# Cluster logits of batches 1 to 3 in paired columns, their low halves added by ScalarE and VectorE

## The chip, the cores and the metric

The program runs on one NeuronCore of a Trainium2 chip. The core has a matrix engine (TensorE, PE in the profile; its weight loads are shown apart as PEld), a vector engine (VectorE, DVE), a scalar engine (ScalarE, ACT), GpSimd (POOL) and a queue engine that issues transfers (SyncE, SP). All work in order, each on its own stream, and wait for one another through semaphores. The metric is the device time of one execution in microseconds, taken as a median of runs.

## The reference

```python
batch, n_heads, seq, head_dim = (4, 8, 768, 64); n_clusters = 16; n_tokens, d_model, d_ff = (3072, 512, 2048)

q_assign = np.argmax(np.einsum('bhsd,hcd->bhsc', q_n, c_n), axis=-1)   # q_n, k_n, c_n: rows scaled to unit norm
k_assign = np.argmax(np.einsum('bhsd,hcd->bhsc', k_n, c_n), axis=-1)
mask = q_assign[:, :, :, None] == k_assign[:, :, None, :]
scores = np.where(mask, scale * np.matmul(q, k.transpose(0, 1, 3, 2)), -1000000000.0)
attn = np.exp(scores - np.max(scores, axis=-1, keepdims=True))
attn = attn / (np.sum(attn, axis=-1, keepdims=True) + 1e-09)
x = np.matmul(attn, v)                          # heads side by side: 3072 tokens of 512
h = x @ w_in
P = a[0] + a[1] * h + a[2] * h ** 2 + a[3] * h ** 3
Q = 1.0 + np.abs(b[0]) * np.abs(h) + np.abs(b[1]) * h ** 2
out = (P / (Q + 1e-6)) @ w_out
```

Every row of q and of k is given to the nearest of its head's 16 centroids, and attention runs only between rows of one cluster. The products of rows and centroids, of which the largest is taken, are called logits here.

## The kernel before

All large products are made from 16-bit halves: a number is kept as a high part and a low part, and a product as two or three matmuls. The work goes by batch (4), by pair of heads (4 a batch) and by block of two tiles of 128 rows (3 a pair). For each pair `prep` loads q, k and v, scales and splits them (`tq1`, `tk1`), turns them by DMA or TensorE (`sq`, `sk`), makes the logits (`ptl`), finds each row's cluster and writes it as a mask into a second operand (`tq2`, `tk2`, turned into `sq`, `sk` again). `attend` then makes 12 score tiles `s` a pair (rows of 128 queries by 768 keys): four matmuls (L1277), the maximum on VectorE (L1292), the exponential and the copy `ah` on ScalarE (both by the helper at L546), the low half of `ah` on VectorE (L1312), a DMA that turns it (`at`), and 18 matmuls into `px` (L1331) for each. Batch 0 goes by keys instead (`z`, `at`, `px` at L1487 to L1512). `moe` works through a block of 256 tokens: `ph` (12 matmuls of 256 columns for each 128 of d_ff, L1639), a chain of elementwise steps on three engines (`u`, `t`, `s` again, a big buffer of that name), and `po` (6 matmuls of 512 columns, L1750).

Attention of batch b is woven into `moe` of batch b-1, and `moe` of batch 3 ends the program alone. The order is not found at run time: `ORDER` holds for each engine the list of operations by number, worked out beforehand; the plan only hands out buffers in that order. So an engine that waits holds up all that stands behind it in its list.

PSUM, into which TensorE writes, has eight banks, shared out in three rings. Ring `s` has two slots of two banks each, for score tiles. Ring `m` has two slots of one bank, for `ph`, `px`, the logits and small sums. Ring `o` has one slot of two banks, for `po`. A slot comes free when the last reader of its tile is done.

The logits of a pair (`logits`, L1158) are 48 matmuls into one `m` slot: for each of 24 tiles of 128 rows one of 16 columns with the centroids' high part, and one of 16 columns that adds the low part to it in PSUM. Behind them stand on VectorE the maximum `mx` (L1189) and the comparison `df` (L1190), which are the readers of the slot; a product on GpSimd (L1193), a second maximum (L1198) and a comparison (L1199) follow in SBUF. The tile `df` has one buffer. `wide_`, an older variant in `prep`, is off.

Of the kernel before, what the change touches and what calls it, by code (L numbers as in the profile page):

```python
# [10 lines left out]
F32 = mybir.dt.float32  # L11
F32R = mybir.dt.float32r
F16 = mybir.dt.float16
# [3 lines left out]
ALU = mybir.AluOpType  # L17
# [10 lines left out]
K = {'ghd': 0.0, 'rvp': 0, 'look': 62.89, 'mulp': 0.4, 'sub': 0, 'xn': 14, 'NR': 8, 'sgp': 1, 'scp': 1, 'vsc': 0.75, 'sup0': 0, 'stk': 2, 'lop': 0, 'mgp': 0, 'rvn': 2, 'tq2': 2, 'at': 3, 'es': 4, 'vn': 2, 'ah': 5, 'rel': 0, 'twin': 1, 'pet': '_01', 'avs': 3, 'ksum': 1, 'fst': '_0', 'hpa': 1}  # L28
# [348 lines left out]
def clustered_attention_moe_kernel(  # L377
# [66 lines left out]
    def kn(name, default=0.0):  # L444
        return K.get(name, default)

# [496 lines left out]
    def prep(b, hp, vt):  # L943
# [192 lines left out]
        for x in ("k1", "q1"):  # L1136
            turn(x, vt + kc("p2", b, 2), by_pe)

        G = 4 * NT
        wide_ = bool(kn("lgw", 0))  # L1140
        ptl = misc([P, G, NCL], F32, f"ptl{n}") if not wide_ else None
        if wide_:
            halves = [misc([P, G // 2, 2, NCL], F32, f"ptl{x}{n}") for x in "qk"]
# [725 lines left out]
```

## Time and profile before

| what | us |
|---|---|
| time, median of 3 runs (lowest, highest) | 896.92 (894.39, 898.39) |
| time of the profiled execution | 897.27 |
| its span, first to last instruction | 895.4 |
| TensorE busy, share of the span | 849.1, 95% |
| VectorE | 785.8, 88% |
| ScalarE | 755.2, 84% |
| GpSimd | 629.3, 70% |

The span is what the trace covers; the time holds 1.9 us more around it. The share is an average over unlike stages: the start (weights and batch 0, with little for TensorE to overlap), the woven stage of batches 1 to 3, and the last `moe`. So the profile is read stage by stage: how long each engine is busy there, and for whom TensorE waits.

### The profile page before, as it was taken

How to read it: one execution, taken by the hardware profiler on the slowest of the kernel's cores; microseconds unless marked ns; L12 is line 12 of the kernel's file. 1: busy time of each engine (PE TensorE's matmuls, PEld its weight loads, DVE VectorE, ACT ScalarE, POOL GpSimd, SP SyncE). 2: the span in 40 equal slices, each digit the busy share in tenths (PEclk: the TensorE clock that was granted, in tenths of full speed). 3: DMA queues.
4: the chain of work that ended last, by engine and by line, in shares of the span. 5: the costliest groups of instructions: out<-in, count | busy, mean ns of one | idle time of the engine just before them, and what ended most of it. 6: DMA issues, size and time to landing. Idle time of an engine off the chain costs nothing.

```text
span 895.4 us, 22725 instructions
## 1 busy us (share of the span) xinstructions
PE 849.1 (95%) x9045; PEld 597.8 (67%) x9045; DVE 785.8 (88%) x1388; ACT 755.2 (84%) x1050; POOL 629.3 (70%) x661
## 2 busy tenths in 40 slices
PE   2789999898999999999999999999999999999998
PEld 2557666675766777567776767777677666766664
DVE  7998979689989899999989998999889888876786
ACT  7557786899999989988999999998988898766674
POOL 1354685699988898778898988789988877422331
PEclk9899999999999999999999999999999999999999
DMA  8478755747989889999999799969888866300000
GB/s 278 138 170 198 190 161 144 206 96 145 194 166 217 159 163 213 188 191 197 167 220 175 154 186 179 180 133 214 144 159 126 160 126 113 87 1 25 7 25 25
DMA packets 364395, 134.70 MB, mean 150 GB/s; under 512 B 342144, under 2 KB 358528, under 8 KB 364288
## 3 DMA queue, kind: packets, MB, share of 16 engines
q1 hardware_dynamic: 364288, 133.24, 73.7%
q8 instruction: 71, 1.16, 0.5%
q14 instruction: 36, 0.29, 0.1%
HBM read 41.98 MB, written 6.29 MB: 54 GB/s over the span
## 4 chain that ended last, share of the span: by engine, by line
PE 55%; DVE 16%; ACT 11%; DMA 6%; issue 5%; POOL 5%; SPq 0%; ACTq 0%; DVEq 0%; POOLq 0%
PE po L1750 19%; PE ph L1639 17%; PE s L1277 6%; PE px L1331 5%; DVE top L1435 3%; ACT s L546 3%; DVE s L1292 3%; ACT u L546 2%; PE px L1506 2%; DVE ah L1312 2%; ACT ah L546 2%; PE z L1487 2%; DVE s L1732 1%; PE s L1408 1%; DMA rwi<-in_moe_w_in_dram 1%
## 5 line engine op out<-in xcount | busy, mean ns | idle before, releaser
L1639 PE MATMUL ph<-x,win 128*128 128x256 f16 x2304 | 267.6, 273 | 2.8 <-DVE xf L1357 1.2
L1750 PE MATMUL po<-wout,u 128*128 128x512 f16 x1152 | 268.6, 379 | 0.0
L1639 PEld LDWEIGHTS <-win 128*128 128x128 f16 x2304 | 223.2, 98 | 43.2 <-DVE xf L1357 3.5
L1679 POOL TENSOR_TENSOR s<-s,u 128x512 f32<-128x512 f32 x96 | 129.0, 1362 | 94.2 <-issue 52.6
L1750 PEld LDWEIGHTS <-u 128*128 128x128 f16 x1152 | 110.5, 98 | 115.3 <-issue 0.5
L1312 DVE SCALAR_TENSOR_TENSOR ah<-s,ah 128x768 f16<-128x768 f32 x144 | 136.1, 952 | 23.7 <-ACT ah L546 22.5
L1292 DVE TENSOR_SCALAR_CACHE_REDUCE s<-s,cc 128x768 f32<-128x768 f32 x144 | 145.2, 1019 | 9.3 <-PE s L1277 8.8
L546 ACT ACTIVATE s<-s,nm 128x768 f32<-128x768 f32 x144 | 125.4, 873 | 21.2 <-DVE s L1292 19.0
L1277 PE MATMUL s<-sk,sq 128*128 128x384 f16 x576 | 116.5, 329 | 4.1 <-DVE ah L1312 3.4
L546 ACT ACTIVATE ah<-s 128x768 f16<-128x768 f32 x144 | 115.9, 810 | 3.1
L1702 POOL TENSOR_TENSOR s<-s,u 128x512 f32<-128x512 f32 x72 | 102.0, 1429 | 16.9 <-ACT u L546 16.5
L1739 POOL TENSOR_TENSOR u<-s,u 128x512 f16<-128x512 f32 x72 | 86.4, 1207 | 30.9 <-DVE s L1732 14.5
L1331 PEld LDWEIGHTS <-at 128*128 128x128 f16 x2592 | 88.5, 98 | 13.6 <-issue 2.2
L1331 PE MATMUL px<-vhi,at 128*128 128x65 f16 x1728 | 91.1, 194 | 1.3 <-DMA at<-ah 0.8
L1331 PE MATMUL px<-vlo,at 128*128 128x64 f16 x864 | 86.8, 192 | 0.0
L1277 PEld LDWEIGHTS <-sq 128*128 128x128 f16 x576 | 52.9, 98 | 41.6 <-DVE ah L1312 8.7
L1660 DVE TENSOR_TENSOR t<-ph,t 128x512 f32<-128x512 f32 x96 | 65.4, 684 | 12.2 <-ACT t L546 11.7
L546 ACT ACTIVATE u<-ph 128x512 f32<-128x512 f32 x96 | 56.9, 595 | 21.8 <-PE ph L1639 21.3
L1732 DVE SCALAR_TENSOR_TENSOR s<-s,t 128x1024 f32<-128x1024 f32 (+1 forms) x49 | 63.0, 1286 | 1.4 <-POOL t L1716 0.6
L546 ACT ACTIVATE u<-t 128x1024 f16<-128x1024 f32 (+1 forms) x49 | 50.9, 1039 | 11.0 <-DVE t L1722 6.0
L546 ACT ACTIVATE t<-ph,gk 128x512 f32<-128x512 f32 x72 | 55.3, 774 | 0.0
L1665 DVE SCALAR_TENSOR_TENSOR t<-t,gk,ph 128x512 f32<-128x512 f32 x72 | 53.0, 742 | 1.1
(219 smaller groups left out, 1466.6 us busy)
## 6 DMA issues: line engine op xcount, KB each, us to landing
rwi<-in_moe_w_in_dram SPq DMA_DIRECT2D x16, 512.0 KB, 4.9
rwo<-in_moe_w_out_dram SPq DMA_DIRECT2D x16, 512.0 KB, 4.8
rk<-in_k_dram SPq DMA_DIRECT2D x32, 192.0 KB, 3.5
rq<-in_q_dram SPq DMA_DIRECT2D x32, 192.0 KB, 3.6
rvm<-in_v_dram SPq DMA_DIRECT2D x16, 384.0 KB, 4.1
rv<-in_v_dram SPq DMA_DIRECT2D x16, 384.0 KB, 4.6
out_dram<-ob SPq DMA_DIRECT2D x11, 512.0 KB, 3.8
at<-ah SPq DMA_TRANSPOSE x144, 4.1
```

Of the source, the lines that this page charges most:

```text
L546: lambda: nc.scalar.activation(out=out(), in_=in_(), func=func, **{a: (x() if callable(x) else x) for a, x in kw.items()}),
L1277: nc.tensor.matmul(sc.ap[:, i, :SH], lhsT=st["q" + x].ap[:, j, t, :], rhs=st["k" + x].ap[:, j, ks, :].rearrange("p t c -> p (t c)"), start ...
L1292: lambda nm=nm, view=view: ts(out=view(), in0=view(), scalar1=cc.ap, scalar2=None, op0=ALU.mult, op1=ALU.min, accum_out=nm.ap),
L1312: lambda part=part, view=view: stt(out=part(1), in0=view(), scalar=A_SCALE, in1=part(0), op0=ALU.mult, op1=ALU.subtract),
L1331: nc.tensor.matmul(px.ap[:, i, :w_], lhsT=at.ap[:, p_, kt, :], rhs=vv.ap[:, j, kt, :w_], start=(kt == 0 and vv is vhi and p_ == 0), stop=( ...
L1639: nc.tensor.matmul(ph[i].ap[:, fi * TW : (fi + 1) * TW], lhsT=win[f // 4][:, wpart, c, f % 4 * P : (f % 4 + 1) * P], rhs=xs[c].ap[:, xpart ...
L1660: lambda i=i, th=th, ph=ph: tt(out=th[i].ap, in0=ph[i].ap, in1=th[i].ap, op=ALU.mult),
L1679: lambda i=i, sh=sh, uh=uh: nc.gpsimd.tensor_tensor(out=sh[i].ap, in0=sh[i].ap, in1=uh[i].ap, op=ALU.mult),
L1702: lambda i=i, sh=sh, uh=uh: nc.gpsimd.tensor_tensor(out=sh[i].ap, in0=sh[i].ap, in1=uh[i].ap, op=ALU.mult),
L1732: lambda tw=tw, sw=sw: stt(out=sw(), in0=sw(), scalar=2.0, in1=tw(), op0=ALU.subtract, op1=ALU.mult),
L1739: lambda i=i, sh=sh, gl=gl, g16=g16, e=(nc.vector if gld else nc.gpsimd): e.tensor_tensor(out=gl[i].ap, in0=sh[i].ap, in1=g16()[:, 0, i * ...
L1750: nc.tensor.matmul(po[ti].ap, lhsT=g16()[:, part, c0 : c0 + P], rhs=wout[f // 4][:, wpart, f % 4], start=(k == 0 and f == f_first), stop=( ...
```

## The change

For batches 1 to 3 (`lgb`), each of the 24 tiles has one matmul of 32 columns instead of two of 16: its moving operand holds the high and the low part of the centroids side by side, and both results lie side by side in PSUM. The sum that PSUM made by itself is now made by two new steps: ScalarE copies the 384 low halves out of PSUM into the buffer of `df` as 16-bit numbers, and VectorE adds them to the high halves, in place in PSUM. The maximum and the comparison read the sums there, every second group of 16.

The tile grows from one bank to two and moves from ring `m` to ring `s`, the one of the score tiles. Batch 0 stays as it was. The variant `wide_` goes, and all five lists of `ORDER` are new.

```diff
-K = {..., 'hpa': 1}
+K = {..., 'hpa': 1, 'lgb': '123'}
...
-        ptl = misc([P, G, NCL], F32, f"ptl{n}") if not wide_ else None
+        paired = str(b) in kn("lgb", "")
+        if paired:
+            ptl = bank([P, 2, 512], F32, "s", f"ptl{n}", 2)
+        else:
+            ptl = misc([P, G, NCL], F32, f"ptl{n}")
+
+        def parts(i):
+            return ptl.ap[:, :, : G * NCL].rearrange("p x (g s c) -> p x g s c", s=2, c=NCL)[:, :, :, i]
+
+        def sums_():
+            return parts(0) if paired else ptl.ap.rearrange("p (x g) c -> p x g c", x=2)
...
         def logits():
             for g, (x, part) in enumerate((("q1", 1), ("q1", 1), ("k1", 2), ("k1", 2))):
                 for t in range(NT):
+                    if paired:
+                        nc.tensor.matmul(
+                            ptl.ap[:, g // 2, (g % 2 * NT + t) * 2 * NCL : (g % 2 * NT + t + 1) * 2 * NCL].rearrange("p (s c) -> p s c", s=2),
+                            lhsT=st[x].ap[:, g % 2, t, :], rhs=cen.ap[:, 0 : part + 1 : part, h0 + g % 2, :],
+                            start=True, stop=True,
+                        )
+                        continue
                     for i in (0, part):
...
-            op("PE", 1205, logits, [cen, st["q1"], st["k1"]], [ptl], vt + kc("p25", b, 2.5), [df], chain="logits")
+        u = vt + kc("p25", b, 2.5)
+        op("PE", 645 if paired else 1205, logits, [cen, st["q1"], st["k1"]], [ptl], u, [df], chain="logits")
+        if paired:
+            act(ac(384, 0, True), lambda: over_rows(df.ap).bitcast(F16), lambda: parts(1), AF.Copy, [ptl], [df], u)
+            dve(465, lambda: tt(out=parts(0), in0=parts(0), in1=over_rows(df.ap).bitcast(F16), op=ALU.add), [df], [ptl], u)
...
-        dve(465, lambda: nc.vector.tensor_reduce(out=mx.ap, in_=ptl.ap, axis=AX.X, op=ALU.max), [ptl], [mx], u)
-        dve(463, lambda: tt(out=df.ap, in0=ptl.ap, in1=spread(mx), op=ALU.is_ge), [ptl, mx], [df], u)
+        dve(465, lambda: nc.vector.tensor_reduce(out=mx.ap.rearrange("p (x g) -> p x g", x=2), in_=sums_(), axis=AX.X, op=ALU.max), [ptl], [mx], u)
+        dve(463, lambda: tt(out=over_rows(df.ap), in0=sums_(), in1=over_rows(spread(mx)), op=ALU.is_ge), [ptl, mx], [df], u)
```

How the new lists stand shows at the logits of batch 2's second pair of heads (`ptl_1`). In the names the first number is the pair of heads (for `ph`, `po` and `u` the block of tokens), the last one only numbers the buffer; L1158 is L1160 in the new file, L1277 is L1273, L1292 is L1288.

TensorE there, before; the logits stand right ahead of a score tile, and the `ph` behind it takes the other `m` slot:

```order
L1158 MATMUL ptl_1_5990<-cen,sq_1_5869 128x16
...
L1158 MATMUL ptl_1_5990<-cen,sk_1_5884 128x16
...
L1277 MATMUL s_0_0_1_6049<-sk_0_5240,sq_0_5483 128x384
...
L1639 MATMUL ph_0_4_0_6057<-x_0_0_3689,win_120 128x256
...
L1277 MATMUL s_0_1_0_6106<-sk_0_5240,sq_0_5483 128x384
```

and now, a `ph` and a `po` standing between the logits and the next two score tiles:

```order
L1160 MATMUL ptl_1_5877<-cen,sq_1_5772 128x32
...
L1160 MATMUL ptl_1_5877<-cen,sk_1_5757 128x32
...
L1635 MATMUL ph_0_4_0_5906<-x_0_0_3675,win_120 128x256
...
L1746 MATMUL po_2_1_5708<-wout_126,u_2_12_5359 128x512
...
L1273 MATMUL s_0_0_1_5945<-sk_0_5156,sq_0_5172 128x384
...
L1273 MATMUL s_0_1_0_5955<-sk_0_5156,sq_0_5172 128x384
```

Both score tiles moved behind `ph` and `po`; the logits are now a third guest of the two slots that they share.

ScalarE at the same place, now; the copy of the low halves is the row `df_1`:

```order
L547 ACTIVATE ah_3_5_1_5777<-s_3_5_1_5744 128x768
L547 ACTIVATE u_0_0_5664<-s_0_0_5723 128x1024
L547 ACTIVATE u_0_0_5664<-u_0_0_5664 128x1024
L547 ACTIVATE df_1_5920<-ptl_1_5877 128x384
L547 ACTIVATE s_0_0_0_5782<-s_0_0_0_5782,nm_0_0_0_5874 128x2x384
L547 ACTIVATE ah_0_0_0_5936<-s_0_0_0_5782 128x768
```

It stands behind two steps of `moe` over 1024 columns and ahead of the exponential of the score tile that was written before the logits.

VectorE at the same place, before:

```order
L1292 TENSOR_SCALAR s_0_0_0_5892,nm_0_0_0_5985<-s_0_0_0_5892,cc_0_5012 128x2x384
L1351 TENSOR_SCALAR inv_3_1_6042<-px_3_1_5903 128x4
L1354 RECIPROCAL inv_3_1_6042<-inv_3_1_6042 128x4
L1357 TENSOR_TENSOR xf_3_1_6046<-px_3_1_5903,inv_3_1_6042 128x256
L1189 TENSOR_REDUCE mx_1_6054<-ptl_1_5990 128x24
L1190 TENSOR_TENSOR df_1_6072<-ptl_1_5990,mx_1_6054 128x384
L1292 TENSOR_SCALAR s_0_0_1_6049,nm_0_0_1_6075<-s_0_0_1_6049,cc_0_5012 128x2x384
L1312 SCALAR_TENSOR_TENSOR ah_0_0_0_6070<-s_0_0_0_5892,ah_0_0_0_6070 128x768
```

and now, with the addition at L1179:

```order
L1288 TENSOR_SCALAR s_0_0_0_5782,nm_0_0_0_5874<-s_0_0_0_5782,cc_0_4940 128x2x384
L1347 TENSOR_SCALAR inv_3_1_5904<-px_3_1_5792 128x4
L1350 RECIPROCAL inv_3_1_5904<-inv_3_1_5904 128x4
L1353 TENSOR_TENSOR xf_3_1_5923<-px_3_1_5792,inv_3_1_5904 128x256
L1179 TENSOR_TENSOR ptl_1_5877<-ptl_1_5877,df_1_5920 128x2x12x16
L1185 TENSOR_REDUCE mx_1_5928<-ptl_1_5877 128x24
L1186 TENSOR_TENSOR df_1_5920<-ptl_1_5877,mx_1_5928 128x384
L1308 SCALAR_TENSOR_TENSOR ah_0_0_0_5936<-s_0_0_0_5782,ah_0_0_0_5936 128x768
L1288 TENSOR_SCALAR s_0_0_1_5945,nm_0_0_1_5961<-s_0_0_1_5945,cc_0_4940 128x2x384
```

The addition is put ahead of the maximum, the three readers of the slot stand together, and `ah` of the earlier score tile changes places with the maximum of the later one.

## Rows read from the trace of the kernel before

**Rows 1.** The page's first part: busy us, share, instructions of each engine.

```profile
PE 849.1 (95%) x9045; PEld 597.8 (67%) x9045; DVE 785.8 (88%) x1388; ACT 755.2 (84%) x1050; POOL 629.3 (70%) x661
```

**Rows 2.** Windows: stretch, its length, then busy us (instructions) of each engine.

```profile
0.00:200.00 200.00, 168.69 (x2035) 123.44 (x2035) 172.70 (x390) 151.84 (x253) 114.83 (x166) 0.98 0.65 176
200.00:400.00 200.00, 191.40 (x2132) 134.67 (x2121) 186.33 (x320) 185.50 (x253) 172.69 (x171) 0.99 0.96 180
350.00:400.00 50.00, 46.62 (x564) 33.00 (x562) 48.84 (x88) 46.30 (x63) 38.19 (x45) 1.00 1.06 190
400.00:760.00 360.00, 357.98 (x3902) 252.64 (x3901) 326.33 (x559) 329.22 (x439) 304.15 (x297) 1.00 0.91 165
760.00:895.40 135.40, 131.03 (x992) 87.01 (x990) 100.45 (x122) 88.67 (x108) 37.60 (x30) 1.00 0.11 29
```

**Rows 3.** The chain in order of time: start us, length us, what, and how many.

```profile
742.44 1.30 PE s L1277 x8
743.74 2.20 PE px L1331 x72
...
690.56 1.31 PE ph L1639 x12
...
859.84 5.24 PE ph L1639 x48
...
880.68 10.37 PE po L1750 x48
```

**Rows 4.** Windows, of the logits' line L1158 alone: PE busy (matmuls), PEld.

```profile
200.00:400.00 200.00, 5.40 (x192) 5.33 (x192) 0.99 0.96 180
400.00:760.00 360.00, 8.10 (x288) 7.92 (x288) 1.00 0.91 165
```

**Rows 5.** Timeline from 526 us: start, length, engine, line, what, [idle before].

```profile
526.37 0.75 PE L1158 MATMUL ptl<-cen,sq 128*128 128x16 f16 x24
526.97 0.75 PE L1158 MATMUL ptl<-cen,sk 128*128 128x16 f16 x24
527.57 1.45 PE L1750 MATMUL po<-wout,u 128*128 128x512 f16 x6
527.76 0.56 DVE L1189 TENSOR_REDUCE mx<-ptl 128x24 f32<-128x384 f32 x1
528.35 0.56 DVE L1190 TENSOR_TENSOR df<-ptl,mx 128x384 bf16<-128x384 f32 x1
```

**Rows 6.** Timeline from 573 us, the same columns.

```profile
573.70 0.74 PE L1158 MATMUL ptl<-cen,sq 128*128 128x16 f16 x24
...
577.08 0.55 DVE L1190 TENSOR_TENSOR df<-ptl,mx 128x384 bf16<-128x384 f32 x1
```

**Rows 7.** Groups of instructions: shapes, count | busy us, mean ns of one | idle before.

```profile
L546 ACT ACTIVATE rs<-px 128x256 f32<-128x256 f32 x12 | 4.5, 378 | 0.2 <-PE px L1549 0.2
L546 ACT ACTIVATE u<-ph 128x512 f32<-128x512 f32 x96 | 56.9, 595 | 21.8 <-PE ph L1639 21.3
L546 ACT ACTIVATE u<-u 128x1024 f32<-128x1024 f32 x47 | 49.5, 1054 | 0.9
L1190 DVE TENSOR_TENSOR df<-ptl,mx 128x384 bf16<-128x384 f32 x16 | 8.9, 555 | 0.3
L1660 DVE TENSOR_TENSOR t<-ph,t 128x512 f32<-128x512 f32 x96 | 65.4, 684 | 12.2 <-ACT t L546 11.7
```

**Rows 8.** Who TensorE waited for, whole span: us in total, times, longest.

```profile
PE vt L812 <- DVE vm L810: 2.5, 1, 2.5
PE ph L1639 <- DVE xf L1357: 1.2, 3, 0.7
PE ph L1639 <- DVE df L1190: 0.6, 1, 0.6
```

**Rows 9.** The same, from 200 to 760 us alone.

```profile
PE s L1277 <- DVE ah L1312: 3.4, 8, 0.9
PE px L1549 <- DVE rs L1541: 3.1, 1, 3.1
```

More of the change, by code (lines that the diff above doesn't have):

```diff
@@ L25 @@
 M_BIG, M_MID, M_LOW = 2.0 ** 15, 2.0 ** 7, 2.0 ** -4
-K = {'ghd': 0.0, 'rvp': 0, 'look': 62.89, 'mulp': 0.4, 'sub': 0, 'xn': 14, 'NR': 8, 'sgp': 1, 'scp': 1, 'vsc': 0.75, 'sup0': 0, 'stk': 2, 'lop': 0, 'mgp': 0, 'rvn': 2, 'tq2': 2, 'at': 3, 'es': 4, 'vn': 2, 'ah': 5, 'rel': 0, 'twin': 1, 'pet': '_01', 'avs': 3, 'ksum': 1, 'fst': '_0', 'hpa': 1}
+K = {'ghd': 0.0, 'rvp': 0, 'look': 62.89, 'mulp': 0.4, 'sub': 0, 'xn': 14, 'NR': 8, 'sgp': 1, 'scp': 1, 'vsc': 0.75, 'sup0': 0, 'stk': 2, 'lop': 0, 'mgp': 0, 'rvn': 2, 'tq2': 2, 'at': 3, 'es': 4, 'vn': 2, 'ah': 5, 'rel': 0, 'twin': 1, 'pet': '_01', 'avs': 3, 'ksum': 1, 'fst': '_0', 'hpa': 1, 'lgb': '123'}
 ORDER = {
     "ACT": """
[32 rows of a table removed]
[33 rows of a table added]
 """,
     "DVE": """
[37 rows of a table removed]
[37 rows of a table added]
 """,
     "PE": """
[28 rows of a table removed]
[28 rows of a table added]
 """,
     "POOL": """
[21 rows of a table removed]
[21 rows of a table added]
 """,
     "SP": """
[13 rows of a table removed]
[13 rows of a table added]
 """,
@@ L1139, in prep, with over_rows @@
         G = 4 * NT
-        wide_ = bool(kn("lgw", 0))
-        ptl = misc([P, G, NCL], F32, f"ptl{n}") if not wide_ else None
-        if wide_:
-            halves = [misc([P, G // 2, 2, NCL], F32, f"ptl{x}{n}") for x in "qk"]
-            def wide_logits(i):
-                x = ("q1", "k1")[i]
-                for g in range(2):
-                    for t in range(NT):
-                        nc.tensor.matmul(
-                            halves[i].ap[:, g * NT + t], lhsT=st[x].ap[:, g, t, :], rhs=cen.ap[:, 0 : 2 + i : 1 + i, h0 + g, :],
-                            start=True, stop=True,
-                        )
+        paired = str(b) in kn("lgb", "")
[7 more added lines that the diff above has]
+            return parts(0) if paired else ptl.ap.rearrange("p (x g) c -> p x g c", x=2)
+        def over_rows(a):
+            return a.rearrange("p (x g) c -> p x g c", x=2)
         def logits():
@@ L1165, in prep @@
         oh = df
-        if wide_:
-            ptl = buf([P, G, NCL], F32, "lsm", f"lsm{n}", 1)
-            for i, x in enumerate(("q1", "k1")):
-                op("PE", 610, lambda i=i: wide_logits(i), [cen, st[x]], [halves[i]], vt + kc("p25", b, 2.5), [df, ptl], chain="logits" + x)
-                low = buf([P, G // 2, NCL], F32, "lsl", f"lsl{x}{n}", 2)
-                act(
-                    ac(192, 0, True), lambda low=low: low.ap, lambda i=i: halves[i].ap[:, :, 1], AF.Copy, [halves[i]], [low],
-                    vt + kc("p3", b, 3),
-                )
-                op(
-                    "DVE", 290,
-                    lambda i=i, low=low: tt(
-                        out=ptl.ap[:, i * 2 * NT : (i + 1) * 2 * NT], in0=halves[i].ap[:, :, 0], in1=low.ap, op=ALU.add
-                    ),
-                    [halves[i], low], [ptl], vt + kc("p3", b, 3), co=[ptl], lock=False,
-                )
-        else:
-            op("PE", 1205, logits, [cen, st["q1"], st["k1"]], [ptl], vt + kc("p25", b, 2.5), [df], chain="logits")
+        u = vt + kc("p25", b, 2.5)
[3 more added lines that the diff above has]
+            dve(465, lambda: tt(out=parts(0), in0=parts(0), in1=over_rows(df.ap).bitcast(F16), op=ALU.add), [df], [ptl], u)
         def spread(m):
```

263 rows, old and new, of the table ORDER are left out of this document.

## The prediction

> **What bounds the kernel now.** The first view is the page's busy shares [rows 1]: TensorE is busy 849.1 of 895.4 us, VectorE 785.8, ScalarE 755.2. That alone settles nothing, since a share mixes stages, so the second view is the busy time by stage [rows 2]. TensorE is idle 200 - 168.69 = 31.3 us in the first 200 us, 8.6 us from 200 to 400, 2.0 us from 400 to 760 and 4.4 us after that. VectorE has 13.7 and 33.7 us idle in the two middle stretches, ScalarE 14.5 and 30.8. So from 200 us on TensorE sets the pace, and hardest from 400 on; only around 350 to 400 is VectorE ahead of it, at 48.84 of 50 us against 46.62.
>
> A busy TensorE could still hide waits, as its matmuls overlap. The chain in order of time tells that it does not [rows 3]: twelve `ph` matmuls take 1.31 us at 690 us, among attention, and 48 take 5.24 us, again 1.31 for twelve, at 860 us, where nothing else runs. A matmul removed from 400 to 760 us is therefore time removed, as long as nothing else becomes late.
>
> Where TensorE did wait there is the third view: between 200 and 760 us 3.4 us in 8 waits for `ah` of a score tile, which is a wait for a slot of ring `s`, and once 3.1 us for batch 0's `rs` [rows 9]. Over the whole span `ph` waited 0.6 us for `df` and 1.2 us in three waits for `xf` [rows 8]; these are waits for a slot of ring `m`, which the logits and `px` share with `ph`.
>
> **The logits.** In one look at them, 24 matmuls on q begin at 526.37, 24 on k at 526.97, and the next `po` at 527.57 [rows 5]: 1.20 us for 48, 25.0 ns each. Windows over their line agree, with 48 matmuls in 1.35 us of busy time, overlap at the end included [rows 4]. The trace has no matmul of 32 columns. Its bounds are the 25.0 ns of 16 columns and the 18 matmuls of 64 or 65 columns of `px`, 2.20 us for 72 or 30.6 ns each [rows 3]. I take a straight line between them, 26.8 ns, which is near the lower end as 32 is nearer to 16. Then 24 matmuls take 0.64 us, between 0.60 and 0.73, and a pair saves 1.20 - 0.64 = 0.56 us, between 0.47 and 0.60. Twelve pairs: **-6.7 us** (-5.6 to -7.2). By the Trainium skill, "TensorE: Matmul & The Clock Gate", section "Back-to-back issue gap", all widths from 1 to 64 columns cost the same floor of about 25 ns; by that the twelve would save 7.2 us, and the sum would come out 0.5 us lower. The 16-column row agrees with the rule, the row of 64 and 65 columns does not.
>
> **The two new steps.** ScalarE's copy of 384 numbers out of PSUM lies between 378 ns for 256 and 595 ns for 512 [rows 7]; on the line between them 0.49 us, 5.8 us for twelve. VectorE's addition has the shape of the comparison that reads 384 numbers from PSUM, 555 ns, and is under the 684 ns of 512 [rows 7]: 0.56 us, 6.7 us for twelve (up to 8.2). Neither stands on TensorE's path by itself. They are covered by `ph` and `po` that TensorE has in its list, and by the idle time named above: ScalarE's 45 us and VectorE's 47 us between 200 and 760. I cost them at nothing there; without the cover they cost up to their own length, which is the rivals' matter. Queued behind the copy are, at the place shown in the section on the change, the exponential and the copy `ah` of a score tile, so each comes up to 0.49 us later, and behind the addition that tile's low half.
>
> **Ring m gets a guest less.** The wait of `ph` for `df`, 0.6 us, was one for the slot of the logits [rows 8] and goes. The 1.2 us behind `xf` are the other slot's, and may shrink or not. I take **-0.6 us** (0 to -1.8).
>
> **Ring s gets a guest more.** The logits now hold a score slot until the comparison is done. Before, they held theirs from 526.37 to 528.35 + 0.56 = 528.91, 2.5 us [rows 5], where VectorE came at once, and from 573.70 to 577.63, 3.9 us [rows 6], where it was busy. The matmuls are 0.56 us shorter, copy and addition 0.49 + 0.56 longer, and the hand-over that is added takes the 0.04 us that lie between the last logit's end at 527.72 and the maximum at 527.76 [rows 5]: 0.53 us more, so 3.1 to 4.5 us. The new list gives so much room: at the place shown, 0.64 us of logits, a `ph` of 1.31, a `po` of 10.37 / 8 = 1.30 and a score tile of 1.30 / 2 = 0.65 [rows 3] stand until the next tile that needs the slot, 3.9 us. Counted in this way for the eleven logits that stand behind the first `ph`, seven have 3.7 to 4.0 us, one 4.3 and three 5.2 to 6.6; the twelfth lies at the end of batch 0 and belongs to the last term. The seven overrun by nothing at the short hold and by 0.6 at the long one, and I take 0.25 each, nearer the short one, as the three readers now stand together in VectorE's list: 7 x 0.25 = **+1.8 us** (0 to 4.2).
>
> **The new lists elsewhere.** All work is the same, and the start (loads, weights, batch 0) is only shuffled by a few places on each queue, SP's loads of q, k and v among them. TensorE's 31.3 idle us there may move either way. One wait won or lost is 2.5 us, as the one for `vm` [rows 8]: **0** (-2.5 to +2.5).
>
> **The sum.** 897.27 - 6.7 - 0.6 + 1.8 = 891.8 us against the profiled execution, which stands 0.35 us above the median of the runs; against the median 891.4. I predict **891.5 us**, 0.6% less. All low ends together give 885.4, all high ends 898.4.
>
> **Rivals.**
>
> *A, the sum holds:* 887.5 to 892.4. For it speaks the 2.0 us of idle time from 400 to 760, where six of the twelve logits lie (288 / 48 [rows 4]).
>
> *B, VectorE and ScalarE take back the gain of the middle.* From 200 to 400 us they are at 93%, and TensorE is not at its end there. The four logits of that stretch (192 / 48 [rows 4]) then save nothing, +2.2 us, and the four additions land on the path, +2.2: 891.8 + 4.4 = 896.2 us, no change that can be told. For it speaks the stretch from 350 to 400 [rows 2]; against it that TensorE's waits from 200 to 760 sum to only a few us.
>
> *C, the score slots decide, and it is slower.* ScalarE works in order, and its list shows the copy behind two steps of `moe` over 1024 columns, 1.05 us each [rows 7]. If the copy must wait for one of them every time, the hold is 4.5 + 1.05 = 5.6 us, the seven narrow places overrun by 1.7 us each, and 11.9 us are added where 7.3 are gained: 897.3 - 7.3 + 11.9 = 901.9 us. It decides from a hold of 3.9 + 7.3 / 7 = 4.9 us. Against it: TensorE's slot waits before were 8 in all and at most 0.9 us [rows 9], under a list of the same kind.
>
> *D, TensorE is not the bound at all.* Its weight loads are busy 67% and VectorE 88% [rows 1]; were VectorE the limit, the shorter logits would save nothing and the 6.7 us of additions would come on top: 897.3 + 6.7 = 904 us. The equal spacing of `ph` with and without attention [rows 3] speaks against it. The Trainium skill, "Perfetto Trace Analysis", section "Identifying the Most-Contended Engine", asks to judge TensorE by the share of its weight loads and not by that of its matmuls, which is this reading; the trace does not agree, by the same spacing.
>
> That 32 columns with two pieces of 16 cost as much as two matmuls, so that nothing is saved, gives 897.3 - 0.6 + 1.8 = 898.5 us; it counts with B.
>
> **Chances.** A 0.50, B 0.34, C 0.13, D 0.03. A measurement of this kernel can tell about 0.5%, 4.5 us, from no change, so faster is below 892.4 and slower above 901.4: faster 0.50, same 0.34, slower 0.16. The range of 8 in 10 goes from 887.5 to 901.0: it holds A and B, leaves out C and D (0.16) and some 0.03 below, where every term takes its low end; the high ends of the sum lie inside it.
>
> **What would show it.** Right: in the changed kernel's trace the 24 matmuls of a pair fill about 0.64 us, TensorE's busy time is 842 us, and its idle time from 200 us on is 15 to 17 us as before; `ph` waits for no `df`. The copy reads 0.49 us and the addition 0.56. B shows as idle time of TensorE between 200 and 400 us grown by 2 us and more, with VectorE over 95% there. C shows as waits of `s` L1273 for the comparison `df` or for `ah`, more than 7 us in all. A new wait in the first 200 us, or a gain there, would be the lists' doing and not the logits'. The forecast is wrong if TensorE's busy time falls by under 5 us or its idle time changes by more than 4.

## The result and the profile after

The changed kernel takes 905.17 us (median of 6 runs, 904.37 to 907.88) against 896.01 for the kernel before beside it: 1.0106 times as long, with a 95% interval of 1.0084 to 1.0127. It is 1.1% slower, where 0.6% faster was forecast, and it lies above the forecast range of 887.5 to 901.0 us.

The profiled execution took 905.08 us, its span is 903.3. The page's busy line, in the columns of [rows 1]:

```profile
PE 847.0 (94%) x8757; PEld 589.5 (65%) x8757; DVE 795.7 (88%) x1400; ACT 757.5 (84%) x1062; POOL 624.8 (69%) x661
```

TensorE's busy time fell by 2.1 us, where 6.7 were expected, and its idle time rose from 46.3 to 56.3. The stages show where, as in [rows 2]:

```profile
0.00:200.00 200.00, 165.26 (x1927) 119.89 (x1929) 173.82 (x384) 146.47 (x246) 110.59 (x163) 0.98 0.66 178
200.00:400.00 200.00, 189.10 (x2050) 130.49 (x2047) 185.97 (x321) 185.90 (x258) 171.27 (x168) 0.98 0.90 173
400.00:760.00 360.00, 353.73 (x3734) 246.08 (x3733) 331.21 (x567) 329.51 (x445) 299.31 (x297) 1.00 0.91 165
760.00:903.30 143.30, 138.90 (x1053) 93.03 (x1051) 104.71 (x131) 95.65 (x117) 43.62 (x35) 1.00 0.17 35
```

The idle time is 34.7, 10.9, 6.3 and 4.4 us, so 3.4, 2.3, 4.3 and 0 more than before. All three added amounts lie ahead of 760 us, the middle one and the last where TensorE had been taken for the limit.

What was forecast of the single steps came out. The logits of the second pair of heads, from the timeline (start, length, engine, line, what):

```profile
192.56 0.45 PE L1160 MATMUL ptl<-cen,sq 128*128 128x32 f16 x12
192.86 0.45 PE L1160 MATMUL ptl<-cen,sk 128*128 128x32 f16 x12
193.16 1.47 PE L1635 MATMUL ph<-x,win 128*128 128x256 f16 x12
```

24 matmuls of 32 columns fill 193.16 - 192.56 = 0.60 us, 25.0 ns each: as much as one of 16 columns [rows 5], so a pair saves 0.60 us and twelve 7.2. The two added steps, from the groups of instructions (count, busy us, mean ns, idle before):

```profile
L547 ACT ACTIVATE df<-ptl 128x384 f16<-128x384 f32 x12 | 5.9, 491 | 3.9 <-PE ptl L1160 3.9
L1179 DVE TENSOR_TENSOR ptl<-ptl,df 128x384 f32<-128x384 f32 x12 | 6.7, 559 | 1.3 <-ACT df L547 1.0
```

They have the lengths that the nearest rows gave, 0.49 and 0.56 us. What did not come out is who TensorE waits for, from 200 to 760 us (us in total, times, longest):

```profile
PE s L1273 <- DVE ah L1308: 7.4, 13, 1.4
PE kb L494 <- ACT tk L547: 2.1, 2, 1.5
PE ph L1635 <- DVE xf L1353: 1.5, 3, 0.7
PE px L1327 <- DVE t L1661: 1.3, 5, 0.4
...
PE ptl L1160 <- DVE inv L1350: 0.9, 1, 0.9
PE ptl L1160 <- DVE ah L1308: 0.8, 2, 0.5
```

The wait for a slot of ring `s` grew from 3.4 us in 8 to 7.4 in 13 [rows 9]. No `ph` waits for `df` any more. The last two rows are new: the logits themselves now wait, 0.8 us of it for `ah`, the last reader of a score slot. The sum had no term for that.

The delay builds up in pieces. Start of a `ph` matmul in the changed kernel less that of the same matmul before (the first of all, then a choice from every 144th):

| started before at, us | 180 | 223 | 273 | 319 | 366 | 422 | 513 | 565 | 608 | 702 | 849 |
|---|---|---|---|---|---|---|---|---|---|---|---|
| later by, us | 4.0 | 4.6 | 2.5 | 3.0 | 5.8 | 7.0 | 6.5 | 8.2 | 8.9 | 8.7 | 7.9 |

The first 4 us arise at the end of batch 0, where two waits stand, the first ahead of the first paired logits:

```profile
162.36 0.45 PE L1160 MATMUL ptl<-cen,sq 128*128 128x32 f16 x12 [1.75 <-ACT at L547]
...
182.90 1.01 PE L1545 MATMUL px<-rs,pick 128*128 128x128 f32 x4 [2.41 <-DVE rs L1537]
183.70 4.19 PE L1635 MATMUL ph<-x,win 128*128 128x256 f16 x24
```

Behind the second, 24 `ph` matmuls take 4.19 us; the chain of before has 2.78 for 24. The windows tell why: the granted clock is 0.53, so nearly all of the stretch runs at 1.2 instead of 2.4 GHz, after a stretch in which TensorE was busy for 0.59 of 3.00 us.

```profile
180.40:183.40 3.00, 0.59 (x4) 0.50 (x4) 3.00 (x2) 1.14 (x2) 2.90 (x5) 0.96 0.83 149
183.40:186.80 3.40, 3.40 (x19) 2.50 (x18) 2.61 (x5) 1.87 (x3) 3.40 (x5) 0.53 1.06 270
```

The kernel before has such a place too: a wait of 3.1 us for `rs` [rows 9], and a granted clock of 0.66 from 205 to 210 us.

### The profile page after: what moved, and what is told of

It reads as the page before. It is cut to its first block, busy times and chain, and to the rows that moved or that the text cites. A ratio compares the mean times of both kernels' runs of the same rounds, so it can differ in the third digit from the quotient of the medians.

```text
span 903.3 us, 22146 instructions
## 1 busy us (share of the span) xinstructions
PE 847.0 (94%) x8757; PEld 589.5 (65%) x8757; DVE 795.7 (88%) x1400; ACT 757.5 (84%) x1062; POOL 624.8 (69%) x661
## 4 chain that ended last, share of the span: by engine, by line
PE 37%; DVE 26%; ACT 19%; issue 8%; POOL 5%; DMA 4%; SPq 1%; DVEq 0%; ACTq 0%; POOLq 0%
PE ph L1635 13%; PE po L1746 13%; ACT s L547 6%; ACT u L547 4%; ACT ah L547 4%; DVE s L1288 4%; DVE top L1431 4%; DVE ah L1308 3%; PE s L1273 3%; PE px L1327 3%; DVE s L1728 2%; DVE t L1656 2%; ACT t L547 1%; POOL s L1675 1%; DMA rwi<-in_moe_w_in_dram 1%
## 5 line engine op out<-in xcount | busy, mean ns | idle before, releaser
L1675 POOL TENSOR_TENSOR s<-s,u 128x512 f32<-128x512 f32 x96 | 128.7, 1358 | 104.2 <-ACT s L547 57.2
L1288 DVE TENSOR_SCALAR_CACHE_REDUCE s<-s,cc 128x768 f32<-128x768 f32 x144 | 145.5, 1017 | 5.1 <-PE s L1273 4.9
L1273 PE MATMUL s<-sk,sq 128*128 128x384 f16 x576 | 116.7, 328 | 8.3 <-DVE ah L1308 7.4
L1698 POOL TENSOR_TENSOR s<-s,u 128x512 f32<-128x512 f32 x72 | 105.5, 1478 | 16.6 <-ACT u L547 16.4
L1735 POOL TENSOR_TENSOR u<-s,u 128x512 f16<-128x512 f32 x72 | 84.1, 1176 | 39.2 <-DVE s L1728 22.2
L1273 PEld LDWEIGHTS <-sq 128*128 128x128 f16 x576 | 51.9, 98 | 50.9 <-DVE ah L1308 15.9
```

Of the source, the lines that this page charges most:

```text
L1273: nc.tensor.matmul(sc.ap[:, i, :SH], lhsT=st["q" + x].ap[:, j, t, :], rhs=st["k" + x].ap[:, j, ks, :].rearrange("p t c -> p (t c)"), start ...
L1288: lambda nm=nm, view=view: ts(out=view(), in0=view(), scalar1=cc.ap, scalar2=None, op0=ALU.mult, op1=ALU.min, accum_out=nm.ap),
L1675: lambda i=i, sh=sh, uh=uh: nc.gpsimd.tensor_tensor(out=sh[i].ap, in0=sh[i].ap, in1=uh[i].ap, op=ALU.mult),
L1698: lambda i=i, sh=sh, uh=uh: nc.gpsimd.tensor_tensor(out=sh[i].ap, in0=sh[i].ap, in1=uh[i].ap, op=ALU.mult),
L1735: lambda i=i, sh=sh, gl=gl, g16=g16, e=(nc.vector if gld else nc.gpsimd): e.tensor_tensor(out=gl[i].ap, in0=sh[i].ap, in1=g16()[:, 0, i * ...
```

## The experiments

The theory on record is that TensorE sets the pace from 200 us on, so that a matmul removed is time removed, and that the two steps are covered. The rivals are that VectorE or ScalarE has no room for the steps, that ring `s` or the new lists cost the time, and that no single engine sets the pace. All ratios below are against runs of the kernel before on the same chip, made beside them; its median there was 895.95 to 897.56 us. Where a difference in us stands beside a ratio it is one of two medians; the two can differ by up to 0.12%, some 1 us.

### Less and more for TensorE alone, under the old lists

```diff
-                    for i in (0, part):
+                    for i in (0, part) if b == 0 else (0,):
```

> The kernel before with its own lists; for batches 1 to 3 only the 24 matmuls with the centroids' high part are made, the 24 with the low part are left out. No step is added and the tile stays in ring m. It tries the premise of the sum alone: 12 x 24 matmuls of 25.0 ns are 7.2 us less TensorE. Theory 'TensorE bounds': the whole comes back, 896.0 - 7.2 = 889 us (888 to 890.5). Rival 'another engine bounds, or the lists were fitted to the old lengths': 893 to 897 us, and TensorE's idle time grows by what does not come back.

Measured: 898.12 us, 1.0010 (0.9996 to 1.0024). Nothing came back. Its stages:

```profile
200.00:400.00 200.00, 191.38 (x2041) 132.96 (x2034) 187.98 (x324) 187.10 (x256) 174.66 (x172) 0.99 0.99 183
400.00:760.00 360.00, 353.71 (x3745) 247.45 (x3744) 325.73 (x554) 326.06 (x435) 300.78 (x296) 1.00 0.89 163
```

TensorE's waits from 200 to 760 us:

```profile
PE s L1277 <- DVE ah L1312: 5.3, 12, 0.7
PE px L1549 <- DVE rs L1541: 3.1, 1, 3.1
PE ph L1639 <- DVE xf L1357: 2.7, 4, 1.3
```

From 400 to 760 us TensorE is busy 4.3 us less than before and idle 4.3 us more (2.0 before, 6.3 now). The waits of a score tile for `ah` (3.4 us before, 5.3 now) and of `ph` for `xf` (1.2 and 2.7) have taken the place of the matmuls. The `ph` matmuls run 2.0 us ahead of before at 422 us, and have given that back by 702 us.

```diff
+                    for i, (j, first) in enumerate(((0, True), (0, True), (part, False)) if b else ((0, True), (part, False))):
```

> The kernel before with its own lists; for batches 1 to 3 the 24 matmuls with the centroids' high part are made twice, so a pair has 72 matmuls of 16 columns instead of 48. The counterpart of the run that left 24 out and came to the same time. Theory 'TensorE has slack in the woven stage': 12 x 0.60 = 7.2 us are hidden too, 897 to 899 us. Rival 'TensorE ties with the others, so that less does not help but more costs': 902 to 905 us.

Measured: 901.90 us, 1.0059 (1.0038 to 1.0080): 5.4 of the 7.2 us stay. The rival holds: less does not help, more costs.

### The two added steps under the old lists

```diff
+            if b:
+                act(ac(384, 0, True), lambda: df.ap.bitcast(F16), lambda: ptl.ap, AF.Copy, [ptl], [df], zr, scale=0.0)
+                dve(465, lambda: tt(out=ptl.ap, in0=ptl.ap, in1=df.ap.bitcast(F16), op=ALU.add), [df], [ptl], zr)
```

> The kernel before with its own lists, 48 matmuls, tile in ring m; for batches 1 to 3 ScalarE's copy of 384 numbers (scaled by zero) into the buffer of df and VectorE's addition of them to the tile are put in, the copy where the logits end in ScalarE's list, the addition right ahead of the maximum. Theory 'the two steps are covered', as the prediction has them: 896 to 898 us. Rival 'VectorE and ScalarE have no room for them': the additions alone are 12 x 0.56 = 6.7 us, so 900 to 903 us, or more with the copies.

Measured: 905.71 us, 1.0089 (1.0068 to 1.0110). Under the old lists the steps are not covered: 8.3 us stay of the 12.7 that they take (5.9 of copies, 6.8 of additions). Which of the two it is, the next two runs ask. The first adds the constant 0 to the tile, an instruction with one operand less and of the same length (0.57 us); the second has the copy alone, not scaled:

> The kernel before with its own lists; for batches 1 to 3 only an addition on VectorE is put in (0 added to the tile of logits, 384 numbers in PSUM, right ahead of the maximum); no copy on ScalarE. The two steps together cost 8.3 us (905.7 against 897.4). Theory 'VectorE is the engine without room': 12 x 0.56 = 6.7 us stay, 903 to 905 us. Rival 'ScalarE is': 897 to 899. Rival 'it is the hand-over between the two, and each alone is small': 898 to 901 us.

Measured: 900.36 us, 1.0036 (1.0024 to 1.0049).

> The kernel before with its own lists; for batches 1 to 3 only the copy on ScalarE is put in (384 numbers of the tile of logits into the buffer of df, which the comparison overwrites); no addition. Theory 'ScalarE is the engine without room': 12 x 0.49 = 5.8 us, 902 to 904 us. Rival 'VectorE is': 897 to 899 us. Rival 'both are, in turn': 899 to 901 us, and the addition alone about as much.

Measured: 900.32 us, 1.0042 (1.0028 to 1.0056). Each costs some 3.9 us, and 0.36 + 0.42 = 0.78% is within the interval of both together. Neither engine is the one without room; both react, as TensorE does.

### The order of the start

Both runs exchange the lists' part ahead of the first logits of batch 1, in which the two programs are the same.

> The kernel before, but every list follows the changed kernel's order up to the first logits of batch 1 (the start and batch 0, where no operation differs), and its own order behind that. Theory 'the new order of the start costs time': the changed kernel's first ph matmuls came 4.0 us later than before, so 896 + 3 to 4 = 899 to 900 us. Rival 'the start is only shuffled', as the prediction has it: 895 to 897 us.

> The changed kernel, but every list follows the order of the kernel before up to the first logits of batch 1, and its own behind that. Theory 'the new order of the start costs time': 905.2 - 3 to 4 = 901 to 902 us. Rival 'the start is only shuffled': 904 to 907 us, the loss lying behind the start.

Measured: 899.57 us, 1.0029 (1.0013 to 1.0045), and 906.34 us, 1.0097 (1.0076 to 1.0119). The new start costs the old kernel some 2.5 us, but taking it out of the changed kernel gives nothing (1.0097 against 1.0106), and in that trace the first `ph` is still 5.6 us late. It is not the cause.

### What is left of the loss without the steps, and without the shorter matmuls

> The changed kernel with its new lists, without ScalarE's copy and VectorE's addition; the low halves lie in PSUM and are left out of the sum. Against the changed kernel (905.2) it shows what the two steps cost under the new lists. Theory 'the two steps carry the loss, and the shorter matmuls give nothing': 905.2 - 8.3 = 897 us. Rival 'the steps carry the loss and the new lists do bring the gain of the matmuls out': 889 to 892 us. Rival 'the new lists or the third guest in ring s carry it': 902 to 905 us.

```diff
-            act(ac(384, 0, True), lambda: over_rows(df.ap).bitcast(F16), lambda: parts(1), AF.Copy, [ptl], [df], u)
-            dve(465, lambda: tt(out=parts(0), in0=parts(0), in1=over_rows(df.ap).bitcast(F16), op=ALU.add), [df], [ptl], u)
```

Measured: 904.88 us, 1.0094 (1.0065 to 1.0123), the changed kernel's time within 0.3 us, with an interval of some 3 us to either side. The loss stays without the steps, and without the copy and the addition for which the logits hold their slot: it is elsewhere. What the steps cost under the new lists is told less surely, as these lists were made with the steps in them, and taking work away gave nothing under the old lists either.

The run with half of the logits' matmuls (1.0010) also has 24 short matmuls a pair and no added step, but the old ring and the old lists. Against it the new ring and lists cost 1.0094 - 1.0010, that is 0.84% or 7.5 us, give or take some 3.

> The changed kernel with its new lists and its tile in ring s, but with the 48 matmuls of 16 columns that sum in PSUM, and so without copy and addition: what is left of the change is the ring and the lists. Theory 'ring and lists cost nothing by themselves': as the run without the two steps, plus 0 to 5.4 us (what 24 matmuls more cost the kernel before): 897 to 902 us. Rival 'ring s or the lists carry the loss': 903 to 908 us.

```diff
                     if paired:
-                        nc.tensor.matmul(... rhs=cen.ap[:, 0 : part + 1 : part, h0 + g % 2, :], start=True, stop=True)
+                        for i in (0, part):
+                            c0 = (g % 2 * NT + t) * 2 * NCL
+                            nc.tensor.matmul(ptl.ap[:, g // 2, c0 : c0 + NCL], ... rhs=cen.ap[:, i, h0 + g % 2, :], start=(i == 0), stop=(i != 0))
```

Measured: 910.42 us, 1.0150 (1.0124 to 1.0177), above both ranges. Ring `s` and the new lists, with the work of the kernel before, cost 14.4 us by the medians and 13.4 by the ratio. A part of this is that the lists were made for shorter logits: against the run above, 24 matmuls more a pair cost 5.5 us of 7.2, about as much as under the old lists (5.4). TensorE's waits for a score slot from 200 to 760 us, in the run without the steps and in this one:

```profile
PE s L1269 <- DVE ah L1304: 7.1, 10, 1.4
PE s L1270 <- DVE ah L1305: 7.8, 10, 1.4
```

They are as long as in the changed kernel, with the steps gone and with either kind of logits. In these two traces the first `ph` is 5.9 and 5.5 us late.

### Ring or lists

Lists made for a tile in ring `s` do not suit one in ring `m`, so the two can be parted only in part. The first run puts ten of the twelve pairs back, the second only the two at the end of batch 0:

```diff
-        paired = str(b) in kn("lgb", "")
+        paired = (b, hp) in {(1, 3), (2, 3)}
```

> The changed kernel's lists, but ten of the twelve pairs of heads make their logits as before: 48 matmuls, tile in ring m, no copy, no addition. Only (batch 1, pair 3) and (batch 2, pair 3) stay as changed. Against the run with the 48 matmuls in ring s (910.4) it tells ring s from the lists. Theory 'the third guest in ring s carries the 14.4 us': 897 to 900 us, TensorE's waits of s for ah back to 3 to 4 us. Rival 'the new lists carry it': 905 to 912 us, and then TensorE's waits show whether ring m, for which these lists weren't made, adds its own (waits of ph or ptl for df).

Measured: 922.44 us, 1.0268 (1.0246 to 1.0289). TensorE's waits from 200 to 760 us:

```profile
PE s L1272 <- DVE ah L1307: 6.6, 10, 1.4
PE ptl L1166 <- DVE t L1660: 3.7, 3, 2.4
PE ph L1634 <- DVE df L1185: 2.8, 2, 1.6
PE ptl L1166 <- DVE inv L1349: 2.2, 1, 2.2
```

Ring `m` adds waits of its own, the three lower rows, so the time tells little. The first row does: with ten of twelve guests gone from ring `s`, its waits are still 6.6 us, near the 7.4 of the changed kernel and not the 3.4 of before. So the guest need not be there for these waits.

The changed kernel's own trace agrees. The logits of a pair hold their slot, from the first matmul to the end of `df`, for 3.1 to 4.6 us, and of the 13 score tiles that wait for `ah` the one nearest to such logits starts 7.2 us after their first matmul, when that slot is free again. No matmul of a score tile waits for `df`; the weight loads do, 2.0 us in 7 places, while TensorE still works on matmuls ahead of them:

```profile
L1273 PEld LDWEIGHTS <-sq 128*128 128x128 f16 x576 | 51.9, 98 | 50.9 <-DVE ah L1308 15.9 <-issue 3.8 <-DVE df L1186 2.0
```

What is left for these waits is the order of the lists; that the guest takes its turn in the two slots is a part of it.

> The changed kernel, but the first two pairs of heads of batch 1, whose logits stand at the end of batch 0 and right behind it, make them as before (48 matmuls, ring m, no added steps). Theory 'ring s at the end of batch 0 costs the first 4 us' (TensorE waited 1.75 us there for a slot ahead of the first logits, and its clock fell): 905.2 - 4 + 2 x 0.6 = 902 us. Rival 'the order there costs it, whatever the ring': 905 to 907 us.

```diff
-        paired = str(b) in kn("lgb", "")
+        paired = (b, hp) in {(1, 2), (1, 3), (2, 0), (2, 1), (2, 2), (2, 3), (3, 0), (3, 1), (3, 2), (3, 3)}
```

Measured: 914.96 us, 1.0174 (1.0144 to 1.0205). The one profiled execution took 906.34 us and the other five 912.46 to 915.94, so its trace does not show the usual case. In it the first `ph` is 0.8 us late instead of 4.0, as the theory says of that place, and at 422 us it is 8.2 late, against 7.0 in the changed kernel: the time won at the end of batch 0 was lost again. But the logits put back wait as well: the first pair 1.80 us for the transfer of `sq`, the second 2.40 us for `t`, a reader of `ph` in ring `m`, and a `ph` behind them 1.59 us for `df`. So the run does not bear out the theory that this place carries part of the loss, and it does not price the place either.

### What sets the pace of the kernel before

These keep the old lists and take work off one engine after another.

> The kernel before with its own lists, except that for batches 1 to 3 the twelve copies of q's 768 high halves (0.78 us of VectorE each) are made by GpSimd, as a step of some 0.9 us in its list. VectorE loses 12 x 0.78 = 9.4 us of work, GpSimd gets 11. Theory 'VectorE is the engine without room': 888 to 892 us. Rival 'all engines tie, and a loop through several of them sets the pace': 896 to 899 us; GpSimd the next to bind: 899 to 903 us.

```diff
-K = {..., 'hpa': 1}
+K = {..., 'hpa': 1, 'hcp': 0.5}
```

Measured: 900.79 us, 1.0045 (1.0029 to 1.0060). The copies take 0.96 us on GpSimd instead of 0.75 on VectorE, and the kernel got slower with this work on an engine that is busy 70%. VectorE's whole busy time fell from 785.8 to 782.1 us.

> The kernel before with its own lists; for batches 1 to 3 the two maxima of a pair on VectorE read one column of each sixteen only, the other fifteen are left out. 24 steps of 0.55 us shrink to about 0.15 us: some 9.6 us less VectorE, nothing more anywhere. Theory 'VectorE is the engine without room': 887 to 890 us. Rival 'the engines tie, so that relief of one alone gives nothing', as with half of the matmuls: 895 to 898 us.

```diff
-tensor_reduce(out=mx.ap, in_=ptl.ap, axis=AX.X, op=ALU.max)
+tensor_reduce(out=mx.ap, in_=ptl.ap[:, :, : 1 if b else NCL], axis=AX.X, op=ALU.max)
-tensor_reduce(out=mx2.ap, in_=df.ap, axis=AX.X, op=ALU.max)
+tensor_reduce(out=mx2.ap, in_=df.ap[:, :, : 1 if b else NCL], axis=AX.X, op=ALU.max)
```

Measured: 895.95 us, 1.0001 (0.9985 to 1.0017). The maxima went from 0.55 to 0.17 and 0.19 us each, some 8.8 us in all. VectorE's whole busy time fell by less, from 785.8 to 782.2 us, as other steps took longer: the comparison L1199 0.73 us instead of 0.61.

> The same, and beside it the 24 matmuls with the low part are left out (7.2 us less TensorE) and ScalarE's sums of squares of q and k read half of their 768 numbers (24 x some 0.32 = 7.7 us less ScalarE), all for batches 1 to 3. Theory 'the engines tie': what gave nothing alone gives together, 887 to 892 us. Rival 'something else sets the pace (the slots, the transfers, GpSimd)': 895 to 898 us.

```diff
-lambda nm=nm: cols(nm + "1", 1).bitcast(BF16), lambda nm=nm: heads(nm), AF.Square,
+lambda nm=nm: cols(nm + "1", 1).bitcast(BF16)[:, : 6 if b else 12], lambda nm=nm: heads(nm)[:, : 6 if b else 12], AF.Square,
-                    for i in (0, part):
+                    for i in (0, part) if b == 0 else (0,):
```

Measured: 896.27 us, 0.9994 (0.9976 to 1.0011). What gave nothing alone gives nothing together, so the theory that these three engines tie falls.

> The kernel before with the joint relief of TensorE, VectorE and ScalarE (896.3, no gain) and GpSimd relieved too: for batches 1 to 3 the product with the weights 1 to 16 is made for one column of sixteen, and in moe the first product of s and u for 384 of 512 columns, for all tokens; the rest is left out. About 12 x 0.85 + 96 x 0.33 = 42 us less GpSimd. Theory 'GpSimd sets the pace': 880 to 890 us. Rival 'the transfers do, or the order itself': 894 to 898 us.

```diff
-out=df.ap, in0=df.ap, in1=w16.unsqueeze(1).broadcast_to([P, G, NCL]), op=ALU.mult
+out=df.ap[:, :, : 1 if b else NCL], in0=df.ap[:, :, : 1 if b else NCL], in1=..., op=ALU.mult
-out=sh[i].ap, in0=sh[i].ap, in1=uh[i].ap, op=ALU.mult
+out=sh[i].ap[:, :384], in0=sh[i].ap[:, :384], in1=uh[i].ap[:, :384], op=ALU.mult
```

Measured: 896.97 us, 0.9988 (0.9975 to 1.0001). GpSimd's busy time fell from 629.3 to 590.5 us and the time by nothing that can be told.

> The same, and the transposes of ah move the high halves only, which px then reads twice; the low halves are left out. Half the bytes of the largest part of the transfers go, whose engines were busy 0.91 to 1.00 from 230 to 690 us. Theory 'the transfers set the pace': clearly under the run before it, 870 to 885 us. Rival 'they do not': as the run before it within 2 us.

```diff
-                        out=at.ap.rearrange("p s k c -> p (s k) c"), in_=ah.ap.rearrange("p s k -> p (s k)"),
+                        out=at.ap.rearrange("p s k c -> p (s k) c")[:, :NT], in_=ah.ap.rearrange("p s k -> p (s k)")[:, :S],
```

Measured: 894.26 us, 0.9966 (0.9952 to 0.9980), 0.2% under the run before it. The transfers' busy share fell from 0.96 and 0.91 [rows 2] to 0.68 and 0.61 in the two stretches, so they are not what holds the kernel.

> As the run with relief of all engines and halved transposes (894.3), and besides VectorE makes the low half of each score tile for 384 of 768 columns only (nobody reads it there): 144 steps of 0.95 us, on which the slot of ring s waits, shrink to about 0.55 us. Some 55 us less VectorE, and a score slot is free 0.4 us earlier. Theory 'the path of a score tile through VectorE and ScalarE sets the pace': TensorE's remaining idle time from 180 to 766 us, some 15 us, largely goes, 880 to 886 us. Rival 'only the order of the lists does': 892 to 895 us.

```diff
-                        out=part(1), in0=view(), scalar=A_SCALE, in1=part(0), op0=ALU.mult, op1=ALU.subtract
+                        out=part(1)[:, :1], in0=view()[:, :1], scalar=A_SCALE, in1=part(0)[:, :1], op0=ALU.mult, op1=ALU.subtract
```

Measured: 887.30 us, 0.9888 (0.9872 to 0.9905), 7.0 us under the run before it and between the two ranges. The row of that step in the kernel before and here, from the groups:

```profile
L1312 DVE SCALAR_TENSOR_TENSOR ah<-s,ah 128x768 f16<-128x768 f32 x144 | 136.1, 952 | 23.7 <-ACT ah L546 22.5
L1313 DVE SCALAR_TENSOR_TENSOR ah<-s,ah 128x384 f16<-128x384 f32 x144 | 78.7, 552 | 36.3 <-ACT ah L546 35.0
```

And the stages here:

```profile
200.00:400.00 200.00, 192.64 (x2100) 135.77 (x2099) 171.90 (x327) 186.18 (x259) 165.57 (x174) 0.99 0.70 134
400.00:760.00 360.00, 358.22 (x3818) 254.36 (x3815) 298.99 (x561) 329.08 (x442) 287.76 (x298) 1.00 0.62 116
```

TensorE's waits from 200 to 760 us, in the run before it and, behind the dots, here:

```profile
PE s L1278 <- DVE ah L1313: 3.6, 7, 1.4
PE ph L1640 <- DVE xf L1358: 3.5, 4, 1.3
PE ph L1640 <- DVE t L1666: 1.8, 2, 1.3
...
PE s L1278 <- DVE ah L1313: 1.7, 4, 0.7
PE s L1278 <- ACT u L546: 1.0, 1, 1.0
PE ph L1640 <- DVE xf L1358: 0.9, 2, 0.5
PE ph L1640 <- DVE t L1666: 0.7, 1, 0.7
```

The step is 0.40 us shorter. TensorE is idle 1.8 us from 400 to 760 us, about as in the kernel before, but now with less work, so all is done earlier. ScalarE keeps its load and VectorE waits for it more. This is the one relief that told clearly. It is the step behind which a score slot comes free, but of the waits for VectorE that went, 1.9 us are the score slot's and 3.7 us those of `ph` for `xf` and `t`. It is also by far the most that was taken off VectorE: its busy time is 780.8 us in the run before and 732.6 here, 48 us less, against 3.6 and 3.7 in the two runs above. No run takes as much off VectorE elsewhere, so whether the place or the amount tells is not shown.

> The same with all 48 matmuls of a pair, 7.2 us more TensorE. Theory 'with the score tiles quicker TensorE is the limit': 7 us over the run before it. Rival 'the order of the lists sets the pace': within 2 us of it.

```diff
-                    for i in (0, part) if b == 0 else (0,):
+                    for i in (0, part):
```

Measured: 890.12 us, 0.9912 (0.9897 to 0.9927), 2.8 us over the run above, again between the two. With the shorter step the 7.2 us of matmuls are worth 2.8.

## Why the prediction was wrong

**The step that failed first is the one that everything rests on:** "a matmul removed from 400 to 760 us is therefore time removed, as long as nothing else becomes late". Something else is late at once. It was read from TensorE's 2.0 us of idle time [rows 2] and from the equal spacing of `ph` with and without attention [rows 3]. Both readings are right and neither proves the step: they say that TensorE is at work, not that the others would keep up if it were quicker. With 7.2 us of its work gone under the old lists, 4.3 us of new idle time stand in that stretch and the time is the same. The page of before held the warning, in the chain of work that ended last, as shares of the span by engine:

```profile
PE 55%; DVE 16%; ACT 11%; DMA 6%; issue 5%; POOL 5%; SPq 0%; ACTq 0%; DVEq 0%; POOLq 0%
```

TensorE is on it for little over half of the time. In the changed kernel it is so for less:

```profile
PE 37%; DVE 26%; ACT 19%; issue 8%; POOL 5%; DMA 4%; SPq 1%; DVEq 0%; ACTq 0%; POOLq 0%
```

Work taken off TensorE, off VectorE at the logits, off three engines or off four at once changed the time by +0.10 to -0.12%, and by -0.34% with the transfers halved too, while work put on cost 3.8 to 8.3 us. This fits an order written for these lengths, in which each engine waits in turn for another; that it is so is argued and not shown. Only the shorter low-half step of the score tiles on VectorE let the rest move up. Both signs that the forecast named for its being wrong came: TensorE's busy time fell by 2.1 us, under 5, and its idle time rose by 10.0, more than 4.

**The logits, -6.7 us.** The length was right within 0.04 us a pair, and the Trainium skill's floor of about 25 ns ("TensorE: Matmul & The Clock Gate", section "Back-to-back issue gap") was nearer than the straight line between rows: 25.0 ns at 32 columns. The worth was wrong: 24 matmuls fewer a pair gave nothing under the old lists. 24 more cost 5.4 us under the old and 5.5 under the new; what taking them away gave within the new lists no run shows.

**The two steps, 0.** Right for the changed kernel as far as can be told: without them it takes 0.3 us less, with an interval of some 3. The cover named for it, TensorE's queued work and the idle time of the two engines, does not explain it: under the old lists the same steps cost 8.3 us beside the same cover. That the new lists leave them room is likely, but a step that is taken out of lists made with it may show nothing in any case.

**Ring `m`, -0.6.** The wait of `ph` for `df` went, as said; the one for `xf` did not shrink (1.2 us before, 1.5 now).

**Ring `s` and the lists elsewhere, +1.8 and 0.** This is the term that was mis-sized. With short logits and no added step on both sides the new ring and lists cost 7.5 us, give or take some 3; with 48 matmuls a pair on both sides 14.4 us, the price of more work in these lists included. So 7 to 14 us stand where 0 to 4.2 and -2.5 to +2.5 were the bounds. The hold itself was sized rightly, 3.1 to 4.6 us where 3.1 to 4.5 was forecast, but it made no matmul of a score tile wait, so the 1.8 us are not found there. What remains is the lists, which were put at nothing. Their bound came from one wait won or lost, but all five were new, and a wait more stands in five places of ring `s` alone, none of them right behind the logits. A sum of such terms closes by itself, as each is a difference of two runs, and proves nothing further. In the recorded sum the low ends are counted from 896.92 and the high ends from 897.27; that is 0.35 us and changes nothing.

**The rivals.** B's sign came by half: TensorE's idle time from 200 to 400 us grew by 2.3 us, but VectorE was busy 186.0 of 200 us there, 93% and not over 95. C foresaw more waits for `ah`, "more than 7 us in all", and they are 7.4. Its mechanism, the longer hold behind the copy, falls: without copy and addition the time and the waits are the same. D gave 904 us, nearest to the time, which is luck: without the additions the changed kernel is no faster, and work taken off VectorE at the logits gives nothing. The rule of the Trainium skill, "Perfetto Trace Analysis", section "Identifying the Most-Contended Engine", which stood beside D, fares better than it did there: judged by weight loads (67% [rows 1]) VectorE is the fullest engine, at 88%, and the one relief that told was on VectorE, though two smaller ones on it (3.6 and 3.7 us of its busy time) gave nothing or cost 0.45%.

**What stays open.** Ring and order could not be parted wholly, as each is made for the other; the waits speak for the order. Which places of the new order cost the time, and why the kernel before gains nothing from less work, is not known. TensorE's busy time fell by 2.1 us where 7.2 us of matmuls went; in windows of 2 us the changed kernel has some 13.6 us at the lower clock and the kernel before some 10.0, which accounts for up to 1.8 of the rest. None of the runs points to a kernel that does the whole work in less time than the one before.

## What to carry to other kernels

An engine that is busy 99% of a stage is a limit only if less work for it makes the stage shorter. Under an order that is fixed beforehand a gain on an engine can be worth nothing while a cost on it is paid; leaving work out in one run, and doubling it in another, tells so before a change is built on it. Where a change replaces a whole order, the order is a term of its own, its bounds are not those of a single wait, and a run with the new order and the old work tells whether it counts.

## What was not expected of the hardware

A matmul of 32 columns took no longer than one of 16, 25.0 ns, where 64 and 65 columns take 30.6 [rows 3]. A gap of 2.41 us on TensorE was followed by a granted clock of 0.53 from 183.4 to 186.8 us, where 24 matmuls took 4.19 us instead of 2.78, so that the gap cost another 1.4 us. And a copy of 768 16-bit numbers that takes VectorE 0.75 us takes GpSimd 0.96.
